# A two-layer attention and MLP kernel: second layer's key sums in one PSUM bank, held exponentials, last rows in the first pair, queries ahead of the last group, later first norm

## The chip, the cores and the metric

The kernel runs on one core of a Trainium2 chip. The metric is the device time of one execution in microseconds (us); the median of three runs stands for a version.

## The reference

Two layers, each of attention and MLP, on one sequence of S = 2048 rows and D = 576 columns, in float32. The attention is linear: queries and keys of H = 32 heads (18 columns each) go through a per-head matrix and two softmaxes, one of the products and one of their negatives.

```
q, k, v = layernorm(x) @ wqkv                     # per head, 18 columns
pq, pk  = q @ w_phi[h], k @ w_phi[h]
phi_q   = concat(softmax(pq), softmax(-pq))       # the same for phi_k
kv, z   = sum_s phi_k^T v, sum_s phi_k            # per head, over all rows
o       = (phi_q kv) / (phi_q z + 1e-6)
x       = x + concat_heads(o) @ wo
x       = x + relu(layernorm(x) @ w1 + b1)^2 @ w2 + b2     # F = 4608
```

This is done twice with the same weights. `kv` and `z` need the keys of all 2048 rows before any query can use them.

## The kernel before

The rows are four blocks of TB = 512, each of NT = 4 tiles of 128. The 576 columns are KC = 4 chunks of 128 and a rest of 64, the 4608 hidden columns NF = 36 groups of 128. Each float32 product is three matmuls on a high and a low part of both operands: ACT makes the high part by a rounding copy, DVE or POOL the low part by a subtraction. So most matmuls wait for a split, a `..h` tile of ACT and a `..l` tile of DVE or POOL.

The stages are these. `g_fold` multiplies wqkv's query and key columns by `w_phi` (tiles `fr`, `fp`, `ft`, `fo`), and the norm of block 0 is woven into it. `g_keys` makes values and keys of each block; `soft_parts`, `soft_exp`, `soft_sums` and `soft_scale` turn a tile of keys into two softmaxes (tile `k_..e`: maxima and minima and half of the differences on DVE, exponential on ACT, sums on DVE, the scaling by POOL, L495); `kv_tile` adds `phi_k^T v` of a tile in 32 small matmuls (L527). At the `barrier`, once all keys are in, `sums_operands` builds from `kv` the matrices with which queries are multiplied: `z`, then `kt` by groups of heads; the last group goes over `kq` (DVE, L580) and two matmuls (L585). Then come the other block's query projections (`g_q`), `g_phi` (sums and scaling of `phi_q`, L643 to L670) and `g_out` (its transposes `t0opt`, L716).

The MLP runs twice on one block (`g_mlp`) and once on a pair of blocks (`g_pair`). In `g_pair`, `products` makes the hidden columns of two blocks with fewer products (PSUM tiles `m_ppx`, `m_ppy`, `m_ppz`) and multiplies the first block's by `w2`; `seconds` does that for the second block in 36 sections of 15 matmuls (numbers 36 to 71: `m_pach`, `m_pacacc`, operands `m_ps` and `m_phc`). In layer 0 the second layer's norm, values and keys of three blocks are woven into `seconds` (`back_keys`; tiles `n_3`, `v_3`, `k_3`, then `_2`, then `_0`).

Eight PSUM banks: two of `ps_w`, and `acc0` to `acc4` and `h`. `wtile` hands out the two, and in turn with them those that `spare["tags"]` lists. For the first eight tiles of layer 1, `kv_tile` uses a `wtile` bank each and ACT or DVE adds it to `kv` (L533, L535); from then on it accumulates in `acc0`.

The code gives engines their work in one order, but a scheduling layer decides how each engine's queue is filled. `weave` runs two generators at a set rate, `held` and `tc.issue_after` keep instructions behind another one. A wait in an engine's queue holds all that stands behind it.

Of the kernel before, what the change touches and what calls it, by code (L numbers as in the profile page):

```python
# [7 lines left out]
F32 = mybir.dt.float32  # L8
# [5 lines left out]
P = 128  # L14
# [7 lines left out]
def layers_kernel(  # L22
# [96 lines left out]
    def paced(gen, cost):  # L119
        for own in gen:  # L120
            yield own if cost is None else cost

# [88 lines left out]
    def g_fold(kpair, vpair):  # L211
# [22 lines left out]
        def turn(k):  # L234
# [15 lines left out]
            nc.vector.tensor_copy(wt[:w, : n * P], pt[:w, : n * P])  # L250
# [84 lines left out]
    def g_norm(x_of, dst, name, then=None, fine=False):  # L335
# [4 lines left out]
        def scale(t):  # L340
            x = x_of(t)
            mv, rstd = moments(x, t, name)
            xn = sb.tile([P, KC * P], F32, tag="xn", name=f"{name}n{t}")
# [29 lines left out]
        def split_rest(h, pt):  # L373
# [3 lines left out]
            nc.vector.tensor_sub(xh[DT:, KC, rows], pt[DT:, : TB // 2], xh[DT:, KC, rows].bitcast(F32))  # L377
# [32 lines left out]
        for half in range(2):  # L410
            for t in range(2):
                apart(half * 2 + t)
                yield 2.2
            yield from pipeline(3, (lambda i: cross(half * 3 + i), lambda i: split(half * 3 + i)), (0.3, 0.6))
# [12 lines left out]
    def project(x, t, w, name):  # L427
# [6 lines left out]
        for k, (a, m) in enumerate(ops):  # L434
            nc.tensor.matmul(pt[:, :HP], a, m, start=(k == 0), stop=(k == len(ops) - 1))
# [73 lines left out]
    def kv_tile(layer, vt, e, name):  # L509
# [7 lines left out]
        first = 0 if layer == 0 else (NB - 2) * NT  # L517
        if n == first:
            st["ps"] = ps_a.tile([P, TB], F32, tag="acc0", name=f"kvp{layer}")
            nc.tensor.matmul(st["ps"][:, : 2 * NS * DH], zero, zeros, start=True, stop=True)  # L520
        stay, last = n >= first, n == NB * NT - 1
        pt = st["ps"] if stay else wtile(f"{name}k")
        po = pt[:, : 2 * NS * DH].rearrange("p (s j f) -> p s j f", s=2, f=DH)
        for j in range(NS):
            for q in range(NQ):
                h = head(q, j)
                nc.tensor.matmul(po[32 * q : 32 * q + 32, :, j], vt[:, h * VW : h * VW + 32],  # L527
                                 e[:, :, h * DH : (h + 1) * DH], start=not stay, stop=True,
                                 tile_position=(0, 32 * q), skip_group_check=True)
        if stay and not last:  # L530
            return
        if (last and first == 0) or n == 0:
            dense["evicted"] = nc.scalar.activation(kv, po, AF.Copy)  # L533
        else:
            nc.vector.tensor_add(kv, po, kv)  # L535

    def sums_operands(layer):
# [28 lines left out]
        for s in range(2):  # L566
# [10 lines left out]
        w = gw[last]  # L577
        own = sb.tile([P, TB], F32, tag="hr", name=f"kq{layer}", bufs=2)
        own = own[:, : 2 * w].rearrange("p (s q f) -> p s q f", s=2, q=NQ)
        nc.vector.tensor_mul(own, kv[:, :, HG].unsqueeze(2).to_broadcast([P, 2, NQ, DH]),  # L580
                             quarter.unsqueeze(1).unsqueeze(3).to_broadcast([P, 2, NQ, DH]))
        pt = wtile(f"kt{layer}2")
# [895 lines left out]
```

## Time and profile before

| | |
|---|---|
| runs | 2551.11, 2557.3, 2559.26 us; median 2557.3 |
| profiled execution | 2557.62 us, its span 2555.9 us |
| PE (TensorE matmul) busy | 2489.1 us, 97% |
| DVE, ACT, POOL busy | 64%, 51%, 38% |
| mean granted TensorE clock | 0.991 |

In the rows of a profile `kv_3k L527 <- POOL k_3K3e L495` means that the instruction of line 527 that writes `kv_3k` stood until POOL's instruction of line 495 that writes `k_3K3e` was done. A row of the timeline has start, duration, engine, line, operation, output <- inputs, shape and count, and in brackets the idle time before it with what ended it. Matmuls of one shape in sequence are merged.

### The profile page before, as it was taken

To read this page: it belongs to the slowest core of one execution; us is meant where nothing else is said; L and a number is where in the kernel's file an instruction comes from. 1 tells how busy PE (TensorE), PEld (TensorE's weight loads), DVE (VectorE), ACT (ScalarE), POOL (GpSimd) and SP (SyncE) were. 2 spreads that over 40 slices of the span, in tenths; PEclk is the share of its full clock that TensorE was granted. 3 is DMA by queue.
4 is the path that set the end of the run, shared out by engine and by line. 5 is a ranking of instruction groups with operands and counts; after the bars stand their busy time and mean duration, and the time that the engine had idled before them with its cause. 6 is when DMAs were issued, how large, how long until landed. Compare 5 with 4: busy or idle time off the path is not lost. (4 is left out here: it accounts for less than half of the span.)

```text
span 2555.9 us, 41504 instructions
## 1 busy us (share of the span) xinstructions
PE 2489.1 (97%) x15108; PEld 2182.6 (85%) x15108; DVE 1634.6 (64%) x2570; ACT 1304.2 (51%) x2293; POOL 971.8 (38%) x1101
## 2 busy tenths in 40 slices
PE   8998999999999999999999989999999999999999
PEld 7998888889888888888889988888888888888888
DVE  7777857555866655555777769484658665555444
ACT  4333555354546666664443435553545466666643
POOL 3544313212335555551434533032123445555322
PEclk9999999999999999999999999999999999999999
DMA  8102432344334433338543133333453344333363
GB/s 252 57 23 72 153 111 83 107 141 165 112 117 126 136 118 98 112 102 265 180 128 115 46 111 110 101 89 107 139 183 90 124 130 144 109 101 104 110 201 128
DMA packets 257224, 312.99 MB, mean 122 GB/s; under 512 B 29818, under 2 KB 175482, under 8 KB 254458
## 3 DMA queue, kind: packets, MB, share of 16 engines
q1 hardware_dynamic: 255760, 307.64, 38.7%
q8 instruction: 118, 1.93, 0.3%
q10 hardware_dynamic: 1258, 2.70, 0.3%
q14 instruction: 88, 0.72, 0.1%
HBM read 255.42 MB, written 54.82 MB: 121 GB/s over the span
## 5 line engine op out<-in xcount | busy, mean ns | idle before, releaser
L1118 POOL TENSOR_TENSOR m_ps<-m_pr,m_ps 128x128 fp32r<-128x128 f32 x144 | 121.9, 847 | 319.2 <-ACT m_ps L1116 264.8
L1117 DVE TENSOR_TENSOR m_ps<-m_pr,m_ps 128x448 fp32r<-128x448 f32 x144 | 93.9, 652 | 153.5 <-ACT m_ps L1116 151.2
L1157 PE MATMUL m_pacc<-m_ps,m_phb 128*128 128x448 f32 x864 | 188.5, 366 | 0.0
L1157 PEld LDWEIGHTS m_pacc<-m_ps,m_phb 128*128 128x128 f32 x864 | 162.2, 188 | 18.0
L1116 ACT ACTIVATE m_ps<-m_pr 128x576 fp32r<-128x576 f32 x144 | 97.9, 680 | 132.3 <-issue 88.5
L1157 PE MATMUL m_pacacc<-m_ps,m_phc 128*128 128x448 f32 x648 | 146.0, 369 | 0.0
L1157 PEld LDWEIGHTS m_pacacc<-m_ps,m_phc 128*128 128x128 f32 x648 | 123.3, 191 | 10.1
L1138 DVE TENSOR_TENSOR m_phb<-m_pz,m_phb 128x512 fp32r<-128x512 f32 x72 | 56.5, 784 | 115.9 <-ACT m_pz L1137 114.4
L820 PE MATMUL m_1ph<-t1onh,m_1h 128*128 128x512 f32 (+1 forms) x380 | 100.7, 390 | 4.5 <-ACT m_1hr L827 2.4
L820 PE MATMUL m_3ph<-t0onh,m_3h 128*128 128x512 f32 (+1 forms) x380 | 98.8, 386 | 2.8 <-ACT m_3hr L827 2.4
L847 PE MATMUL m_2acc<-m_2s,m_2hb 128*128 128x448 f32 x432 | 100.1, 365 | 0.0
L847 PE MATMUL m_0acc<-m_0s,m_0hb 128*128 128x448 f32 x432 | 100.1, 365 | 0.0
L847 PE MATMUL m_3acc<-m_3s,m_3hb 128*128 128x448 f32 x432 | 99.7, 366 | 0.0
L847 PE MATMUL m_1acc<-m_1s,m_1hb 128*128 128x448 f32 x432 | 99.7, 366 | 0.0
L820 PE MATMUL m_0ph<-a_0nh,m_0h 128*128 128x512 f32 (+1 forms) x380 | 97.7, 384 | 0.0
L820 PE MATMUL m_2ph<-a_2nh,m_2h 128*128 128x512 f32 (+1 forms) x380 | 97.7, 384 | 0.0
L847 PEld LDWEIGHTS m_2acc<-m_2s,m_2hb 128*128 128x128 f32 x432 | 81.0, 188 | 10.6 <-ACT m_2hb L828 0.2
L847 PEld LDWEIGHTS m_0acc<-m_0s,m_0hb 128*128 128x128 f32 x432 | 81.0, 188 | 10.7 <-ACT m_0hb L828 0.2
L847 PEld LDWEIGHTS m_3acc<-m_3s,m_3hb 128*128 128x128 f32 x432 | 81.0, 188 | 10.6 <-ACT m_3hb L828 0.2
L847 PEld LDWEIGHTS m_1acc<-m_1s,m_1hb 128*128 128x128 f32 x432 | 81.0, 188 | 10.5
L820 PEld LDWEIGHTS m_1ph<-t1onh,m_1h 128*128 128x128 f32 x380 | 70.2, 193 | 19.2 <-ACT m_1hr L827 3.2
L810 POOL TENSOR_TENSOR m_1s<-m_1r,m_1s 128x128 fp32r<-128x128 f32 x36 | 27.0, 749 | 151.7 <-ACT m_1s L806 134.8
(2504 smaller groups left out, 7464.3 us busy)
## 6 DMA issues: line engine op xcount, KB each, us to landing
m_pr<-in_B_w SPq DMA_DIRECT2D x144, 288.0 KB
m_pr<-in_B_w SPq DMA_DIRECT2D x72, 256.0 KB
hd<-m_pu SPq DMA_DIRECT2D x72, 256.0 KB
m_pg<-hd SPq DMA_DIRECT2D x72, 256.0 KB
m_3r<-in_B_w SPq DMA_DIRECT2D x36, 288.0 KB
m_2r<-in_B_w SPq DMA_DIRECT2D x36, 288.0 KB
m_1r<-in_B_w SPq DMA_DIRECT2D x36, 288.0 KB
m_0r<-in_B_w SPq DMA_DIRECT2D x36, 288.0 KB
```

The lines of the kernel that those rows point to most:

```text
L810: nc.gpsimd.tensor_sub(s2[:, D + R : 2 * D], r2[:, R:], s2[:, R:D].bitcast(F32))
L820: nc.tensor.matmul(ph[:, cols], a, m, start=(k == 0), stop=(k == len(ops) - 1))
L847: nc.tensor.matmul(acc[t][:, :R], a[:, rows], m, start=(f == 0 and k == 0), stop=(f == NF - 1 and k == 2))
L1116: nc.scalar.activation(s2[:, :D], r2, AF.Copy)
L1117: nc.vector.tensor_sub(s2[:, D : D + R], r2[:, :R], s2[:, :R].bitcast(F32))
L1118: nc.gpsimd.tensor_sub(s2[:, D + R : 2 * D], r2[:, R:], s2[:, R:D].bitcast(F32))
L1138: nc.vector.tensor_sub(hl, r, hh.bitcast(F32))
L1157: nc.tensor.matmul(accs[b][t][:, :R], a[:, rows], m, start=(g == 0 and k == 0), stop=(g == NF - 1 and k == 2))
```

## The change

It has seven parts. (1) In layer 1 all key sums accumulate in bank `acc4` from the first tile on, and ACT copies them out once; `acc4` is no longer handed out during `seconds` (behind it, `acc0` is handed out in its place). (2) In `back_keys` the sums of a tile come one tile later (`late`), and a block's last tile after the next block's norm; the norm makes all four tiles' scales first, in buffers of the tag `qk`; `g_features` keeps its exponentials behind the squares. (3) The first two steps of `back_keys`, two tiles of the first norm, are taken before the last rows of `products`. (4) The last group of `sums_operands` comes after all query projections. (5) In the first of the MLP's groups the low part of `m_1s` waits for the norm. (6) At the end of `g_mlp` the next stage's first products come ahead of the last rows. (7) The first norm starts three steps later in the weave, and behind the latest `ft` copy.

```diff
@@ -122,2 +122,6 @@
 
+    def idle(n, gen):
+        yield from (1.0 for _ in range(n))
+        yield from gen
+
     def lagged(n, produce, consume, by=1):
@@ -249,3 +253,3 @@
             wt = sb.tile([GW, TB], F32R, tag="ft", name=f"ft{c}_{i}", bufs=4).bitcast(F32)
-            nc.vector.tensor_copy(wt[:w, : n * P], pt[:w, : n * P])
+            dense["folded"] = nc.vector.tensor_copy(wt[:w, : n * P], pt[:w, : n * P])
             return wt
@@ -342,3 +346,6 @@
             mv, rstd = moments(x, t, name)
-            xn = sb.tile([P, KC * P], F32, tag="xn", name=f"{name}n{t}")
+            if fine:
+                xn = sb.tile([P, D], F32, tag="qk", name=f"{name}n{t}", bufs=5)[:, : KC * P]
+            else:
+                xn = sb.tile([P, KC * P], F32, tag="xn", name=f"{name}n{t}")
             nc.vector.tensor_scalar(xn, x[:, : KC * P], mv[:, 0:1], rstd, op0=ALU.subtract, op1=ALU.mult)
@@ -376,3 +383,4 @@
             nc.scalar.activation(xh[:, KC, rows], pt[:, : TB // 2], AF.Copy)
-            nc.vector.tensor_sub(xh[DT:, KC, rows], pt[DT:, : TB // 2], xh[DT:, KC, rows].bitcast(F32))
+            dense["normed"] = nc.vector.tensor_sub(xh[DT:, KC, rows], pt[DT:, : TB // 2],
+                                                   xh[DT:, KC, rows].bitcast(F32))
 
@@ -409,7 +417,6 @@
 
-        for half in range(2):
-            for t in range(2):
-                apart(half * 2 + t)
-                yield 2.2
-            yield from pipeline(3, (lambda i: cross(half * 3 + i), lambda i: split(half * 3 + i)), (0.3, 0.6))
+        for t in range(NT):
+            apart(t)
+            yield 2.2
+        yield from pipeline(3 * NT // 2, (cross, split), (0.3, 0.6))
 
@@ -434,3 +441,3 @@
         for k, (a, m) in enumerate(ops):
-            nc.tensor.matmul(pt[:, :HP], a, m, start=(k == 0), stop=(k == len(ops) - 1))
+            dense["projected"] = nc.tensor.matmul(pt[:, :HP], a, m, start=(k == 0), stop=(k == len(ops) - 1))
         return pt
@@ -516,9 +523,6 @@
         st["n"] += 1
-        first = 0 if layer == 0 else (NB - 2) * NT
-        if n == first:
-            st["ps"] = ps_a.tile([P, TB], F32, tag="acc0", name=f"kvp{layer}")
+        if n == 0:
+            st["ps"] = ps_a.tile([P, TB], F32, tag=f"acc{KC * layer}", name=f"kvp{layer}")
             nc.tensor.matmul(st["ps"][:, : 2 * NS * DH], zero, zeros, start=True, stop=True)
-        stay, last = n >= first, n == NB * NT - 1
-        pt = st["ps"] if stay else wtile(f"{name}k")
-        po = pt[:, : 2 * NS * DH].rearrange("p (s j f) -> p s j f", s=2, f=DH)
+        po = st["ps"][:, : 2 * NS * DH].rearrange("p (s j f) -> p s j f", s=2, f=DH)
         for j in range(NS):
@@ -527,10 +531,6 @@
                 nc.tensor.matmul(po[32 * q : 32 * q + 32, :, j], vt[:, h * VW : h * VW + 32],
-                                 e[:, :, h * DH : (h + 1) * DH], start=not stay, stop=True,
+                                 e[:, :, h * DH : (h + 1) * DH], start=False, stop=True,
                                  tile_position=(0, 32 * q), skip_group_check=True)
-        if stay and not last:
-            return
-        if (last and first == 0) or n == 0:
+        if n == NB * NT - 1:
             dense["evicted"] = nc.scalar.activation(kv, po, AF.Copy)
-        else:
-            nc.vector.tensor_add(kv, po, kv)
 
@@ -576,15 +576,20 @@
 
-        w = gw[last]
-        own = sb.tile([P, TB], F32, tag="hr", name=f"kq{layer}", bufs=2)
-        own = own[:, : 2 * w].rearrange("p (s q f) -> p s q f", s=2, q=NQ)
-        nc.vector.tensor_mul(own, kv[:, :, HG].unsqueeze(2).to_broadcast([P, 2, NQ, DH]),
-                             quarter.unsqueeze(1).unsqueeze(3).to_broadcast([P, 2, NQ, DH]))
-        pt = wtile(f"kt{layer}2")
-        p3 = pt[:w, : 2 * w].rearrange("p (s n) -> p s n", s=2)
-        for s in range(2):
-            nc.tensor.matmul(p3[:, s], own[:, s].rearrange("p q f -> p (q f)"),
-                             place.rearrange("p q d -> p (q d)"), start=True, stop=True)
-        keep(p3, [k[:w, :, last, :w] for k in (kbh, kbl)])
         sums[layer].update(zb=zb, kb=(kbh, kbl))
 
+        def last_group():
+            w = gw[last]
+            own = sb.tile([P, TB], F32, tag="hr", name=f"kq{layer}", bufs=2)
+            own = own[:, : 2 * w].rearrange("p (s q f) -> p s q f", s=2, q=NQ)
+            nc.vector.tensor_mul(own, kv[:, :, HG].unsqueeze(2).to_broadcast([P, 2, NQ, DH]),
+                                 quarter.unsqueeze(1).unsqueeze(3).to_broadcast([P, 2, NQ, DH]))
+            pt = wtile(f"kt{layer}2")
+            p3 = pt[:w, : 2 * w].rearrange("p (s n) -> p s n", s=2)
+            with tc.issue_after(dense["projected"].ins):
+                for s in range(2):
+                    nc.tensor.matmul(p3[:, s], own[:, s].rearrange("p q f -> p (q f)"),
+                                     place.rearrange("p q d -> p (q d)"), start=True, stop=True)
+            keep(p3, [k[:w, :, last, :w] for k in (kbh, kbl)])
+
+        return last_group
+
 
@@ -688,3 +693,3 @@
         yield from held(pipeline(NT, (start, lambda t: soft_exp(ph[t]), add, factors, lambda t: phi_scale(ph[t], rs[t])),
-                                 (2.6, 0.4, 3.0, 2.8, 1.2)))
+                                 (2.6, 0.4, 3.0, 2.8, 1.2)), ("last", "squared"))
 
@@ -808,2 +813,3 @@
                 nc.vector.tensor_sub(l1, r1, h1.bitcast(F32))
+            with tc.issue_after(dense["normed"].ins) if behind else nullcontext():
                 nc.vector.tensor_sub(s2[:, D : D + R], r2[:, :R], s2[:, :R].bitcast(F32))
@@ -878,2 +884,8 @@
         nc.scalar.activation(yt, acc[KC], AF.Copy)
+        if then:
+            then()
+        for t in range(NT):
+            x = sb.tile([P, D], F32, tag="x", name=f"{name}x{t}", bufs=5)
+            nc.sync.dma_start(x, xm[b][t])
+            after.append(x)
         by_rows(NF - 1, range(2), range(3))
@@ -883,9 +895,2 @@
             nc.tensor.transpose(p3[:, t], yt[:, t * P : (t + 1) * P], ident)
-        for t in range(NT):
-            x = sb.tile([P, D], F32, tag="x", name=f"{name}x{t}", bufs=5)
-            nc.sync.dma_start(x, xm[b][t])
-            nc.vector.tensor_add(x[:, R:], p3[:, t], x[:, R:])
-            after.append(x)
-        if then:
-            then()
         by_rows(NF - 1, range(2, NT), range(3))
@@ -893,2 +898,4 @@
             nc.vector.tensor_add(x[:, :R], acc[t][:, :R], x[:, :R])
+        for t, x in enumerate(after):
+            nc.vector.tensor_add(x[:, R:], p3[:, t], x[:, R:])
             nc.sync.dma_start(out[b * TB + t * P : b * TB + (t + 1) * P] if layer else xs[b][t], x)
@@ -1335,3 +1342,3 @@
         drain(softs)
-        sums_operands(layer)
+        last_group = sums_operands(layer)
         spare["tags"] = [f"acc{i}" for i in range(NC)] + ["h"]
@@ -1344,2 +1351,3 @@
         drain(queries)
+        last_group()
         dst = {}
@@ -1353,3 +1361,3 @@
     vpair = [piece_tiles(f"w0v{h}", TAGS_A) for h in range(2)]
-    weave(g_fold(kpair, vpair), g_norm(load_x(0), xT[0], "n0_0"), 0.5)
+    weave(g_fold(kpair, vpair), idle(3, held(g_norm(load_x(0), xT[0], "n0_0"), ("folded",))), 0.5)
     pending = []
@@ -1405,2 +1413,3 @@
             new_slots("vs")
+            late = []
             for b in order[:3]:
@@ -1410,2 +1419,5 @@
                 yield from g_norm(rows_of(b), xk, f"n{m}", fine=True)
+                while late:
+                    kv_tile(1, *late.pop(0))
+                    yield 0.8
                 if not last:
@@ -1425,6 +1437,10 @@
 
-                stages = (raw, start, lambda t: soft_exp(es[t]), end, lambda t: None)
-                if not last:
-                    stages += (lambda t: kv_tile(1, vts[t], es[t], f"kv{m}_{t}"),)
-                yield from pipeline(NT, stages, (1.0, 2.6, 0.4, 1.8, 0.1, 0.8))
+                def keep_sums(t):
+                    if not last:
+                        late.append((vts[t], es[t], f"kv{m}_{t}"))
+                        if len(late) > 1:
+                            kv_tile(1, *late.pop(0))
+
+                yield from pipeline(NT, (raw, start, lambda t: soft_exp(es[t]), end, keep_sums),
+                                    (1.0, 2.6, 0.4, 1.8, 0.8))
                 if last:
@@ -1440,5 +1456,8 @@
         weave(g_mlp(layer, order[1], nxt, [], f"m{layer}_{order[1]}", None, then), back, 5.0)
-        drain(products)
-        spare["tags"] = ["acc4"]
-        weave(seconds, iter(()) if layer else back_keys(), 4.0)
+        back = iter(()) if layer else back_keys()
+        for k, _ in enumerate(products):
+            if k == NP - 1:
+                next(back, None)
+                next(back, None)
+        weave(seconds, back, 4.0)
         if layer == 0:
@@ -1446,3 +1465,3 @@
             prev, b = order[-2], order[-1]
-            spare["tags"] = ["acc1", "acc2", "acc3", "acc4", "h"]
+            spare["tags"] = ["acc0", "acc1", "acc2", "acc3", "h"]
             x, xprev, vpair = {}, keep["x"], keep["v"]
```

The order that the scheduler makes differs at many places. Three of them follow. Line numbers are those of each kernel (the changed one's are 4 to 7 higher around here).

PE, barrier of layer 0. `t0q2qp` are query projections, `t0opt` the first transposes of `g_out`. Before:

```order
L435 MATMUL t0q2qp_2895<-t0q0h,n_2h 128x288
L435 MATMUL t0q2qp_2895<-t0q0h,n_2l 128x288 x4
L435 MATMUL t0q2qp_2895<-t0q0l,n_2h 128x288 x2
L585 MATMUL kt_2797<-place,kq_2795 72x72 x2
L435 MATMUL t0q2qp_2832<-t0q1h,n_2h 128x288 x5
L435 MATMUL t0q2qp_2832<-t0q1h,n_2l 128x288 x4
```

Now:

```order
L442 MATMUL t0q2qp_2937<-t0q1h,n_2h 128x288 x5
L442 MATMUL t0q2qp_2937<-t0q1h,n_2l 128x288 x4
L442 MATMUL t0q2qp_2937<-t0q1l,n_2h 128x288 x5
L589 MATMUL kt_2955<-place,kq_2953 72x72 x2
L721 MATMUL t0opt_2982<-ident,t0fQ0e 126x128
L721 MATMUL t0opt_2982<-ident,t0fQ1e 126x128
```

The two `kt` matmuls went from the middle of the projections to their end.

PE and DVE in `seconds`, at the end of the second layer's first block of keys. `k_3K3e` is that block's last tile of exponentials, `n_2` the next block's norm, `w_2v` its value weights; numbers 48 and 49 are sections. PE before:

```order
L527 MATMUL kv_3_2k<-k_3K2e,vs_12028 32x2x18 x32
L527 MATMUL kv_3_3k<-k_3K3e,vs_12029 32x2x18 x32
L1157 MATMUL m_pach<-m_ps_48_12670,m_phc_12676 128x448 x3
L1157 MATMUL m_pacacc_11963<-m_ps_48_12670,m_phc_12676 128x448 x3
L1157 MATMUL m_pacacc_11964<-m_ps_48_12670,m_phc_12676 128x448 x3
```

PE now:

```order
L376 MATMUL n_2p_12949<-ident,n_2e 128x128 x2
L1164 MATMUL m_pacacc_12003<-m_ps_49_12772,m_phc_12778 128x448 x3
L1164 MATMUL m_pacacc_12004<-m_ps_49_12772,m_phc_12778 128x448 x3
L1154 MATMUL m_pacacc_12005<-m_phc_12778,m_ps_49_12772 128x512 x3
L362 MATMUL n_2p_12980<-ident,n_2n_12891 128x128 x4
L362 MATMUL n_2p_12987<-ident,n_2n_12904 128x128 x4
L531 MATMUL kvp_12669<-k_3K3e,vs_11923 32x2x18 x32
L1164 MATMUL m_pach<-m_ps_50_12857,m_phc_12863 128x448
```

DVE before:

```order
L1117 TENSOR_TENSOR m_ps_48_12670<-m_pr_48_12668,m_ps_48_12670 128x448
L1202 TENSOR_TENSOR m_phc_12676<-m_pg_12674,m_phc_12676 128x512
L309 TENSOR_TENSOR w_2v0l<-w_2v0r,w_2v0h 128x1440
L309 TENSOR_TENSOR w_2v1l<-w_2v1r,w_2v1h 128x1440
L470 TENSOR_REDUCE k_3K3m<-k_3ks_12624 128x32
L471 TENSOR_REDUCE k_3K3m<-k_3ks_12624 128x32
L474 TENSOR_TENSOR k_3K3e<-k_3ks_12624,k_3K3m 128x576
L1117 TENSOR_TENSOR m_ps_49_12735<-m_pr_49_12733,m_ps_49_12735 128x448
```

DVE now:

```order
L478 TENSOR_REDUCE k_3K3m<-k_3ks_12598 128x32
L481 TENSOR_TENSOR k_3K3e<-k_3ks_12598,k_3K3m 128x576
L351 TENSOR_SCALAR n_2n_12891<-x_2_2_12881,n_2m_12884,n_2d_12885 128x512
L1124 TENSOR_TENSOR m_ps_48_12709<-m_pr_48_12707,m_ps_48_12709 128x448
L1209 TENSOR_TENSOR m_phc_12715<-m_pg_12713,m_phc_12715 128x512
L352 TENSOR_SCALAR n_2e<-x_2_2_12881,n_2m_12884,n_2d_12885 128x128
L334 BN_AGGR n_2m_12897<-n_2s_12896 128x2
L313 TENSOR_TENSOR w_2v1l<-w_2v1r,w_2v1h 128x1440
L490 TENSOR_REDUCE k_3K3r<-k_3K3e 128x64
L1124 TENSOR_TENSOR m_ps_49_12772<-m_pr_49_12770,m_ps_49_12772 128x448
L491 RECIPROCAL k_3K3r<-k_3K3r 128x64
L1209 TENSOR_TENSOR m_phc_12778<-m_pg_12776,m_phc_12778 128x512
```

On PE the sums of the last tile moved from ahead of section 48 to ahead of section 50, behind the next norm's transposes. On DVE the splits of sections 48 and 49 now stand behind three scales `n_2n` (two more come just before the rows shown), and one of the two weight splits, and the key steps.

DVE, start of the kernel. `ft` are copies that the fold's matmuls read, `n_0s` the statistics of the first norm on the loaded `x`. Before:

```order
L250 COPY ft_0_221<-fp_0_216 126x512
L329 BN_STATS n_0s_226<-x_0_0_224 128x6 x2
L250 COPY ft_1_242<-fp_1_237 126x512
L330 BN_AGGR n_0m_227<-n_0s_226 128x2
L250 COPY ft_2_247<-fp_2_244 72x256
```

Now:

```order
L254 COPY ft_0_221<-fp_0_216 126x512
L254 COPY ft_1_228<-fp_1_223 126x512
L254 COPY ft_2_233<-fp_2_230 72x256
L254 COPY ft_0_251<-fp_0_246 126x512
L254 COPY ft_1_268<-fp_1_263 126x512
L277 TENSOR_TENSOR w0k0l<-fo_1_253,w0k0h 128x288
L277 TENSOR_TENSOR w0k1l<-fo_2_270,w0k1h 128x72
L254 COPY ft_2_284<-fp_2_281 72x256
L254 COPY ft_0_303<-fp_0_298 126x512
L333 BN_STATS n_0s_318<-x_0_0_316 128x6
```

The first statistics moved behind six more copies and two splits.

## The prediction

> **What bounds the kernel now.** The page comes first: which engine fills the span.
>
> ```profile
> PE 2489.1 (97%) x15108; PEld 2182.6 (85%) x15108; DVE 1634.6 (64%) x2570; ACT 1304.2 (51%) x2293; POOL 971.8 (38%) x1101
> ```
>
> PE (TensorE) works 2489.1 of 2555.9 us, so at most 66.8 us can be won without taking away a matmul. The change takes away hardly any: only PE's pauses can pay. The table of waits names them (total us, times, longest).
>
> ```profile
> PE kt L585 <- DVE kq L580: 7.4, 2, 4.4
> PE kv_3k L527 <- POOL k_3K3e L495: 6.1, 1, 6.1
> PE kv_3k L527 <- POOL k_2K3e L495: 5.0, 1, 5.0
> PE fo L259 <- DVE ft L250: 3.8, 3, 3.1
> PE m_ppx L1128 <- DVE m_pu L1241: 2.8, 2, 1.4
> PE n_3p L355 <- DVE n_3n L344: 2.3, 1, 2.3
> PE n_0p L355 <- DVE n_0n L344: 2.0, 3, 1.5
> PE a_1qp L435 <- ACT a_1qs L453: 1.5, 1, 1.5
> PE m_1ph L820 <- DVE m_1h L808: 1.4, 1, 1.4
> PE z L547 <- DVE kv L535: 0.8, 1, 0.8
> ```
>
> All but the `a_1qp` row lie where the change moves something; those nine rows sum to 31.6 us. A pause costs more than its length: the table of busy time by stretch (PE, PEld, DVE, ACT, POOL, then the granted clock) shows PE at half clock right after the long ones.
>
> ```profile
> 206.21:209.62 3.41, 3.02 (x14) 3.02 (x15) 3.41 (x9) 0.29 (x1) 0.17 (x1) 0.50 0.75 212
> 1469.14:1472.55 3.41, 3.25 (x15) 3.25 (x16) 3.41 (x10) 0.70 (x2) 0.00 (x0) 0.50 0.00 0
> 1250.68:1254.10 3.42, 3.34 (x70) 3.05 (x71) 2.71 (x5) 0.00 (x0) 1.69 (x3) 0.50 0.44 126
> 1326.79:1332.60 5.81, 5.81 (x77) 5.26 (x78) 2.62 (x5) 0.00 (x0) 1.61 (x2) 0.50 0.61 172
> ```
>
> Work at half clock loses about half its busy time: 1.5, 1.6, 1.7 and 2.9 us, together 7.7.
>
> **The change part by part.**
>
> *Queries ahead of the last group.* In both barriers PE stood before the two `kt` products.
>
> ```profile
> 204.30 2.25 DVE L580 TENSOR_TENSOR kq<-kv,quarter 128x144 f32<-128x144 f32 x1
> 206.60 0.75 PE L585 MATMUL kt<-place,kq 128*72 128x72 f32 x4 [4.38 <-DVE kq L580]
> 213.32 1.68 POOL L662 TENSOR_TENSOR t0fQ1e<-t0fQ1e,t0fQ1r 128x576 f32<-128x576 f32 x1 [0.84 <-DVE t0fQ1r L657]
> 217.95 0.27 PE L716 MATMUL t0opt<-ident,t0fQ0e 128*126 128x128 f32 x1
> 1469.30 0.76 PE L585 MATMUL kt<-place,kq 128*72 128x72 f32 x4 [3.06 <-DVE kq L580]
> 1476.02 1.68 POOL L662 TENSOR_TENSOR t1fQ1e<-t1fQ1e,t1fQ1r 128x576 f32<-128x576 f32 x1 [0.84 <-DVE t1fQ1r L657]
> 1481.16 0.27 PE L716 MATMUL t1opt<-ident,t1fQ0e 128*126 128x128 f32 x1
> ```
>
> The query projections no longer queue behind `kt`, so PE reaches `t0opt` earlier by wait and slow clock, 4.38 + 1.5 = 5.9, at 212.05. What ends last there next is POOL's scaling of `t0fQ1e`, done at 215.00. The 2.25 us `kq` leaves the DVE chain ahead of it, so I put it at 212.75: gain 5.2. In layer 1 `kq` was short, the scaling (1477.70) moves only some 0.3 to 1477.4, and the gain is 1481.16 - 1477.4 = 3.75. Sum **9.0**; if POOL's scaling did not move at all, 2.95 + 3.46 = 6.4; gross, 10.6.
>
> *Held exponentials and the key sums in one bank.* At two block ends PE waited for the last tile's scaled exponentials and got 6.06 + 1.7 and 5.03 + 2.9 us late: 15.7. Now that tile's sums come after the next block's norm, so nothing of it is on PE's way. But DVE was full there too (12.07 of 12.70 us), and it splits the operands of PE's next sections (15 matmuls each, `m_pach` first).
>
> ```profile
> 1232.00:1244.70 12.70, 12.70 (x244) 10.74 (x242) 12.07 (x12) 7.36 (x12) 4.89 (x4) 1.00 0.49 142
> 1235.98 2.64 DVE L1202 TENSOR_TENSOR m_phc<-m_pg,m_phc 128x512 fp32r<-128x512 f32 x1
> 1238.54 1.91 DVE L309 TENSOR_TENSOR w_2v0l<-w_2v0r,w_2v0h 128x1440 fp32r<-128x1440 f32 x1
> 1241.95 0.74 DVE L470 TENSOR_REDUCE k_3K3m<-k_3ks 128x32 f32<-128x576 f32 x1
> 1243.93 1.58 DVE L1117 TENSOR_TENSOR m_ps<-m_pr,m_ps 128x448 fp32r<-128x448 f32 x1
> 1245.44 0.94 DVE L1202 TENSOR_TENSOR m_phc<-m_pg,m_phc 128x512 fp32r<-128x512 f32 x1
> 1246.30 1.34 DVE L483 TENSOR_REDUCE k_3K3r<-k_3K3e 128x64 f32<-128x1152 f32 x1
> 1248.38 2.33 POOL L495 TENSOR_TENSOR k_3K3e<-k_3K3e,k_3K3r 128x1152 f32<-128x1152 f32 x1 [2.54 <-DVE k_3K3r L484]
> 1249.11 2.14 DVE L1202 TENSOR_TENSOR m_phc<-m_pg,m_phc 128x512 fp32r<-128x512 f32 x1
> 1250.76 1.19 PE L527 MATMUL kv_3k<-k_3K3e,vs 128*32 128x36 f32 x64 [6.06 <-POOL k_3K3e L495]
> 1252.34 0.68 DVE L1202 TENSOR_TENSOR m_phc<-m_pg,m_phc 128x512 fp32r<-128x512 f32 x1
> 1256.76 0.55 DVE L344 TENSOR_SCALAR n_2n<-x,n_2m,n_2d 128x512 f32<-128x512 f32 x1 [3.38 <-PE n_2p L355]
> ```
>
> By the new order the split at 1235.98 serves section 47, not 48, and three `n_2n` of 0.55 us stand ahead of section 48's. From 1238.54 on: two `n_2n`, one `w_2v0l` (some 1.9), three key steps of 0.74, a third `n_2n`: 5.8, so `m_ps_48` starts near 1244.3 and `m_phc_48` ends near 1246.2. PE, busy up to 1244.70, wants both there: the sums of tiles 0 to 2 only change places with sections 45 to 47. That returns 1.5. Section 49 hangs on a `w_2v1l`, the 1.34 reduction, two short steps and an `m_phc` that falls on POOL's 2.33 us scaling: 0.68 alone, 2.14 beside POOL, so 0.9 to 2.4 is returned. Midway, about 3.2 of 7.8 comes back; the second block end has the same pieces, and with a little for what a late DVE pushes on I take 7 of 15.7 back and keep **8.7**. Bounds: nothing returned, 15.7; 6.3 returned at each end, 3. The eight DVE additions `kv` (L535) go free. The last one, `z`'s 0.85, becomes an ACT copy behind four matmuls: **0.4** (0 to 0.85).
>
> *Last rows in the first pair.* `n_3n` of two tiles is now made before `last_rows`, so the 2.31 us at `n_3p` go. Its other two tiles now stand ahead of the `m_px` additions, which free the banks for section 36.
>
> ```profile
> 1169.81 1.67 DVE L1183 TENSOR_TENSOR m_px<-m_pacc,m_px 128x448 f32<-128x448 f32 x3
> ```
>
> `x_3_3` is loaded only when `x_3_2`'s buffer is free, and DVE stands before its statistics. I reckon these additions start some 0.6 us later than now and PE waits that long: **1.7** kept (0 to 2.3). Behind that load SP's queue holds the weights of section 38 and `w_3v0r`, wanted two sections and more later; I cost this at nothing, and at the same 0.6 again if that cover is gone.
>
> *MLP parts.* The `m_1h` split moves ahead of `m_1s`: **1.4** (0 to 2.9, if the slow clock behind it goes as well). At the end of `g_mlp` all four tiles' products stand between two `m_ppx` groups, 12 matmuls (the row below has six) and four transposes, where 1.40 + 1.41 us were needed: **2.8** for the two layers (1.4 to 2.8). The exponentials that `g_features` now holds behind the squares cost nothing on an ACT that is 51% busy; if a query tile's sums come late by it, the weave has other matmuls there, and I see no wait on them in the table above.
>
> ```profile
> 855.44 1.40 PE L847 MATMUL m_2acc<-m_2s,m_2hb 128*128 128x448 f32 x6
> 9.80 0.82 DVE L329 BATCH_NORM_STATS2 n_0s<-x 128x6 f32<-128x288 f32 x2 [3.82 <-DMA x<-in_A_x]
> ```
>
> *Later first norm.* DVE stood 3.82 us before the statistics of `x` while the `ft` copies that PE wanted were queued behind them. Six more copies now come first. The waits in this stage beyond kernel start are about 3.8 + 2.0 plus small ones; the norm ends later and may hold the first projections, so I take **4.0** of some 6.6 (-2 to 6.6).
>
> Sum: 9.0 + 8.7 + 0.4 + 1.7 + 1.4 + 2.8 + 4.0 = 28.0. The profiled execution took 2557.62 (span 2555.9 and 1.7 around it), 0.3 above the median; 2557.3 - 28.0 = **2529.3**.
>
> **A rule against a row.** The Trainium skill, page "TensorE: Matmul & The Clock Gate", section "What's actually happening", says the clock halves after at least one idle window of about 3.4 us. The trace is stricter: after the 3.06 us wait at 1469.30, shorter than that, the clock was 0.50. By the rule that place would lose no 1.6 us and layer 1's `kt` would gross 3.06; that is below the 3.75 I take, so the sum would be 27.3 and the time 2530.0.
>
> **The rivals.** *Half of it: DVE and POOL set the pace* (0.20). For it: DVE was 12.07 of 12.70 busy, and its `m_phc` took 2.64 and 2.14 beside POOL's scaling against 0.68 alone. Against it: DVE idled 3.38 us soon after (row at 1256.76). Then `kt` gives 6.4, the block ends 3, `m_ppx` 2.8, the rest nothing: 12.2, or 2545. The Trainium skill, page "SBUF — State Buffer", section "SBUF: two separate sides", has DVE operations with two SBUF inputs and GpSimd ones hold a shared port for a whole instruction, the later one fully blocked. The 2.14 beside a 2.33 agrees; by that rule the larger return (2.4, not 0.9) holds at section 49.
>
> *Slower: two banks instead of three.* `acc4` leaves the rotation in layer 0's second products, so each of the 40 projections (16 values, 24 keys) takes the bank that the last but one left, and needs ACT's eviction. The `a_1qp` row shows one such wait, 1.5 us, though just one in the kernel. Projections in this stage never waited with three banks. At 1.5 each it is 60 us and the time 2557.3 - 28 + 60 = 2589. It decides from 28/40 = 0.7 a projection: 0.08. At 0.5 to 0.9 each (20 to 36) the result is within 0.3% of before: 0.10.
>
> **How the numbers follow.** A measurement of this kernel can tell 0.3%, 7.7 us. Forecast 0.62, half 0.20 (also faster), no change 0.10, slower 0.08: faster 0.82, same 0.10, slower 0.08. My own case runs from the upper bounds (10.6 + 15.7 + 0.85 + 2.3 + 2.9 + 2.8 + 6.6 = 41.8: 2516) to 2543, where half of the sum is left and the half rival starts; that rival's spread reaches 2549. Range 2517 to 2549.
>
> **What would show it.** Right: `kt` gone from the waits, and what is left at `t0opt` under 1 us with POOL as releaser; no `kv_3k` wait; new waits of `m_pach` on DVE `m_phc` or `m_ps` of 2 to 4 us at each block end; clock 1.00 there; `n_3p` under 1 us; no `m_ppx` wait on L1248; `fo` under 1 us. Wrong: `v_2pv` or `k_2kp` waiting for ACT's evictions again and again (two banks), `m_pach` waiting over 5 us at a block end, or the first `v_0pv` waiting for `n_0h`.

## The result

The changed kernel took 2539.8 us (median of five runs, 2535.8 to 2546.4) against 2557.3 for the kernel before: a ratio of 0.9937, 95% interval 0.9917 to 0.9958. The interval excludes 1, so it is faster, as forecast, and it is inside the range; but the gain is 17.5 us and not 28.0. The profiled execution took 2540.98, its span 2539.3.

The first page row and, of the waits of PE in the changed kernel, those that bear on the argument (total us, times, longest):

```profile
PE 2486.9 (98%) x15108; PEld 2183.0 (86%) x15108; DVE 1641.5 (65%) x2562; ACT 1307.5 (51%) x2293; POOL 968.9 (38%) x1101
PE n_2p L376 <- DVE n_2l L371: 5.8, 1, 5.8
PE t1onp L362 <- DVE t1onn L351: 4.4, 4, 2.0
PE m_ppx L1135 <- DVE m_pu L1244: 3.4, 4, 1.4
PE n_0p L362 <- DVE n_0n L351: 2.6, 1, 2.6
PE n_0p L376 <- DVE n_0l L371: 2.1, 1, 2.1
PE t0opt L721 <- DVE t0fQ0e L667: 1.2, 1, 1.2
PE t1opt L721 <- DVE t1fQ0e L667: 1.2, 1, 1.2
PE kt L589 <- DVE kq L583: 1.2, 2, 0.7
```

PE's idle time went from 66.8 to 52.4 us. Gone are both long `kt` waits, the two `kv_3k` waits and `m_1h`. But the longest wait, 5.8 us, is new, and none of the predicted `m_pach` waits is there.

Where the time went is read from when named matmuls start. The table takes the start of one matmul after another in each trace; a negative number is time won in that stretch. The second profile is one of the same kernel, taken later (`x8_after_again`).

| stretch, from the start of one matmul to that of the next | forecast | first profile | second |
|---|---|---|---|
| start to the first `z` of layer 0 (fold, first norm, keys) | -4.0 | +0.3 | +1.8 |
| to the first `m_3acc` (barrier, `kt`, `t0opt`) | -5.2 | -0.7 | -3.6 |
| to the first `m_2acc` (MLP with `g_features` beside it) | 0 | -4.6 | -4.6 |
| to the first `m_pacc` (end of `g_mlp`, `products`) | -1.4 | -1.9 | -1.7 |
| to section 36 | 0 | -0.2 | -0.2 |
| to the first `k_3kp` (last rows, first norm of stage) | -1.7 | -3.2 | -3.0 |
| to the first `n_lastp` (both block ends) | -8.7 | -0.5 | -2.1 |
| to layer 1's last `z` row | -0.4 | -1.6 | -1.6 |
| to the first `m_1acc` (barrier, `kt`, `t1opt`, `m_1h`) | -5.2 | +0.8 | +2.7 |
| to the last `m_1acc` (MLP with `g_features`) | 0 | -4.6 | -4.6 |
| to the end | -1.4 | -0.3 | -0.9 |

So the largest gain, 9.2 us, is one costed at nothing, and the two largest terms, 9.0 and 8.7, brought about 0 to 2 each.

### The profile page after: what moved, and what is told of

Same layout as the page of the kernel before. It is cut to its first block, busy times and chain, and to the rows that moved or that the text cites. A ratio compares the mean times of both kernels' runs of the same rounds, so it can differ in the third digit from the quotient of the medians.

```text
span 2539.3 us, 41497 instructions
## 1 busy us (share of the span) xinstructions
PE 2486.9 (98%) x15108; PEld 2183.0 (86%) x15108; DVE 1641.5 (65%) x2562; ACT 1307.5 (51%) x2293; POOL 968.9 (38%) x1101
## 5 line engine op out<-in xcount | busy, mean ns | idle before, releaser
L853 PEld LDWEIGHTS m_0acc<-m_0s,m_0hb 128*128 128x128 f32 x432 | 80.9, 188 | 10.6 <-ACT m_0hb L834 0.2
L853 PEld LDWEIGHTS m_2acc<-m_2s,m_2hb 128*128 128x128 f32 x432 | 80.9, 188 | 10.6 <-ACT m_2hb L834 0.2
L816 POOL TENSOR_TENSOR m_0s<-m_0r,m_0s 128x128 fp32r<-128x128 f32 x36 | 29.6, 824 | 143.5 <-ACT m_0s L811 127.4
L816 POOL TENSOR_TENSOR m_2s<-m_2r,m_2s 128x128 fp32r<-128x128 f32 x36 | 29.2, 810 | 143.5 <-ACT m_2s L811 136.7
```

The lines of the kernel that those rows point to most:

```text
L816: nc.gpsimd.tensor_sub(s2[:, D + R : 2 * D], r2[:, R:], s2[:, R:D].bitcast(F32))
L853: nc.tensor.matmul(acc[t][:, :R], a[:, rows], m, start=(f == 0 and k == 0), stop=(f == NF - 1 and k == 2))
```

## The experiments

**The gain that was costed at nothing.** In the kernel before, ACT's queue (start, duration; in brackets the idle time before) stood at the exponential of a query tile until POOL had made its input. Behind it stood the squares' first step `m_3hr`, for which PE waited:

```profile
429.67 1.16 ACT L479 ACTIVATE a_0Q3e<-a_0Q3e 128x1152 f32<-128x1152 f32 x1 [6.15 <-POOL a_0Q3e L475]
430.74 0.67 ACT L827 ACTIVATE m_3hr<-m_3ph,b1t 128x512 f32<-128x512 f32 x1
431.46 2.50 PE L820 MATMUL m_3ph<-t0onh,m_3h 128*128 128x512 f32 x5 [2.36 <-ACT m_3hr L827]
431.60:435.00 3.40, 3.40 (x9) 2.68 (x10) 2.58 (x4) 2.16 (x4) 0.90 (x1) 0.51 0.22 64
```

The last row is the table by stretch: 3.4 us at clock 0.51 behind the wait, which costs 1.7 more. Layer 1 has the same at 1697.75. In PE's list of waits before, the two are these rows, which the prediction's table leaves out although it shows shorter ones:

```profile
PE m_1ph L820 <- ACT m_1hr L827: 2.4, 1, 2.4
PE m_3ph L820 <- ACT m_3hr L827: 2.4, 1, 2.4
```

With `("last", "squared")` ACT does the squares first, and in the profile of the changed kernel neither wait nor slow stretch is left. Two runs test this, one without that edit and one with it alone.

`x1_no_exps`: the change without

```diff
-                                 (2.6, 0.4, 3.0, 2.8, 1.2)), ("last", "squared"))
+                                 (2.6, 0.4, 3.0, 2.8, 1.2)))
```

> The changed kernel with one thing undone: g_features no longer keeps its exponentials behind the squares (all else as changed). Theory (ACT's queue): before, the exponential a_0Q3e stood 6.15 us in ACT's queue waiting for POOL, and m_3hr behind it made PE wait 2.36 us in each layer, with a half-clock stretch after it; the changed kernel gained 4.6 us between the 180th and the 300th m_3acc matmul and again 4.6 us at m_1acc in layer 1. So both waits on ACT L833 of about 2.4 us come back, both gains of 4.6 go, and the time is 9 us above the changed kernel's 2540: about 2549. Rival (the pause went because the low split of m_3s was put behind the norm): no wait comes back and the time stays within 2 us of 2540.

2547.1 us, ratio to before 0.9957 (0.9941 to 0.9974), 7.3 above the change. Both waits are back, 2.4 us each, and the two MLP stretches win less than 0.1 us each instead of 4.6:

```profile
PE m_3ph L826 <- ACT m_3hr L833: 2.4, 1, 2.4
PE m_1ph L826 <- ACT m_1hr L833: 2.4, 1, 2.4
```

`x2_exps_alone`: the kernel before with that line alone.

> The kernel before with one edit of the change: g_features holds its exponentials behind the squares. Theory (the exponential of a query tile stood in ACT's queue waiting 6.15 us for POOL, with the squares of the MLP features behind it): both waits of PE on m_3hr and m_1hr, 2.36 us each, go and the 3.4 us of half clock behind each; 4.5 us in each layer, about 9 in all, 2548. Rival, as the prediction had it (these exponentials are worth nothing): 2556 to 2557, and the gain of 5 us between m_3acc's 180th and 300th matmul in the profile of after came from another edit.

2548.5 us, ratio 0.9967 (0.9954 to 0.998): 7.4 us. In its trace the two stretches win 4.6 and 4.7 us. The edit is worth 9.2 in its own stretches and 7 to 7.5 in the medians; that is about 40% of what the whole change brought.

**The new wait at the block end.** The third norm's transposes stood 5.82 us. They need one of the two banks in the rotation, and DVE's split `n_2l` frees it. DVE's queue in the changed kernel, with one row of POOL and PE's row:

```profile
1238.54 2.47 POOL L502 TENSOR_TENSOR k_3K3e<-k_3K3e,k_3K3r 128x1152 f32<-128x1152 f32 x1 [1.18 <-DVE k_3K3r L491]
1238.92 2.37 DVE L351 TENSOR_SCALAR n_2n<-x,n_2m,n_2d 128x512 f32<-128x512 f32 x1
1241.47 1.17 DVE L333 BATCH_NORM_STATS2 n_0s<-x 128x6 f32<-128x288 f32 x3
1242.67 0.76 DVE L333 BATCH_NORM_STATS2 n_0s<-x 128x6 f32<-128x288 f32 x2
1244.86 1.12 DVE L333 BATCH_NORM_STATS2 n_0s<-x 128x6 f32<-128x288 f32 x3
1248.18 1.29 DVE L371 TENSOR_TENSOR n_2l<-n_2p,n_2h 128x512 fp32r<-128x512 f32 x2
1248.93 0.69 PE L376 MATMUL n_2p<-ident,n_2e 128*128 128x128 f32 x2 [5.82 <-DVE n_2l L371]
```

Statistics of the next block (`n_0s`, 3.05 us of eight) and the splits of later sections came before `n_2l`. Ahead of them `n_2n` took 2.37 us beside POOL's scaling of 2.47, where it took 0.55 in the kernel before. Two remedies: give the third bank back, or hold the statistics back.

`x4_three_banks`: the key sums and `spare["tags"]` as in the kernel before.

```diff
+        first = 0 if layer == 0 else (NB - 2) * NT
...
+        spare["tags"] = ["acc4"]
         weave(seconds, back, 4.0)
```

> The changed kernel with the key sums of the second layer's first two blocks made as before, each in a bank of the rotation and added to kv by DVE, so that the rotation has three banks (acc4 back); the held last tile and the late sums stay. Theory (bank): the waits of n_2p and n_0p tail transposes on DVE's n_2l and n_0l (5.82 and 2.12 us in the changed kernel, with half clock after them) go, below 1 us each; the first value projection v_2pv comes 6 us earlier relative to k_3 than in the changed kernel, and 8 to 11 us are won in all: 2529 to 2532. Rival (DVE sets the pace): a wait of 3 us or more at each block end stays, now of m_pach on m_ps or m_phc; the time is 2535 to 2540.

2528.5 us in one run. The 5.8 us became 2.8 and, at the next transposes, 1.2; DVE's addition into `kv` now ends the longer one. The block ends' stretch won 4.5 us.

```profile
PE n_2p L376 <- DVE kv L542: 2.8, 1, 2.8
```

But 4.8 us of its gain lies elsewhere, at layer 1's barrier, which the bank theory doesn't explain; it is taken up below.

`x5_stats_held`: two banks, but

```diff
+            with tc.issue_after(dense["normed"].ins) if fine else nullcontext():
                 mv, rstd = moments(x, t, name)
```

> The changed kernel, still with two banks in the rotation, with the statistics of a block's rows kept behind the last split of the block ahead (in the changed kernel 3.4 us of n_0s statistics stand in DVE's queue ahead of the n_2l that frees the bank). Theory (the bank wait is as long as what DVE does ahead of n_2l): the 5.82 us wait falls by about 3.4 to some 2.4, one half-clock stretch less; 3.5 to 5 us are won at the first block end, less at the second. Rival (the wait hangs on something else, the exponentials' scaling or the splits): it stays above 5 us.

2531.5 us in one run; the block ends win 5.9, and the wait is 2.9 us:

```profile
PE n_2p L377 <- DVE n_2l L372: 2.9, 2, 2.7
```

So the statistics ahead of `n_2l` are at least as good a cause as the bank: without them half of the wait goes, with the bank back about a third. The totals of these two runs hold more than that: at layer 0's barrier, which neither edit touches, they win 5.7 and 5.8 us, against 0.7 and 3.6 in the two profiles of the change.

`x9_banks_and_stats`: both.

> The change with both remedies for the wait of the third norm's transposes: three banks in the rotation, with the key sums kept as before, and the norm's statistics held behind the split that frees a bank. Theory (both take away the same wait, that of n_2p and n_0p on n_2l and n_0l): their gains of about 11 and 8 us do not add, 2525 to 2530. Rival (they are separate gains): 2520 or less.

2526.7 us, ratio 0.9882 (0.9866 to 0.9898): the gains don't add, as expected. The block ends win 6.0 us. At the second one `n_0p` still waits 2.6 us for `n_0l`; what is left of the wait at the first is released by DVE's addition into `kv`:

```profile
PE n_2p L377 <- DVE kv L543: 1.7, 1, 1.7
```

**The barrier.** `x3_kt_early` puts the last group back ahead of the queries:

```diff
-        last_group = sums_operands(layer)
+        sums_operands(layer)()
```

Its two `kt` matmuls also lose the `tc.issue_after` that keeps them behind the projections.

> The changed kernel with the last group of kt put back ahead of the query projections in both barriers. Theory (the gain is given back inside the barrier): PE waits 3 to 4.4 us at kt again, but the second half of g_out (tiles Q2, Q3) hangs on DVE and POOL, which do not start earlier for it; by the first m_3acc matmul of layer 0 the kernel stands within 1 us of the changed one, in layer 1 within 2 us. Rival, the prediction's term: the move is worth 9 us, so 5 us are lost in layer 0 by the first m_3acc and 4 us more in layer 1, time about 2549.

2544.8 us in one run, between the two. In layer 0 this kernel wins 0.9 us in the stretch and in layer 1 it loses 3.0; over both that is 2 to 3 us worse than the two profiles of the change. So inside the change the move is worth 2 to 3 us by the stretches and 5 by the whole time, not 9; 2.0 us of the loss against the first profile lie ahead of layer 0's first `z`, where the edit changes nothing. The `kt` waits grew to 5.7 and 5.8 us, against 4.38 and 3.06 in the kernel before:

```profile
PE kt L588 <- DVE kq L583: 11.4, 2, 5.8
```

So something else in the change had made DVE late here. Layer 1 in the change, POOL, DVE, ACT and PE:

```profile
1446.52 0.41 ACT L535 ACTIVATE kv<-kvp 128x288 f32<-128x288 f32 x1 [0.45 <-PE kvp L531]
1448.20 1.15 ACT L312 ACTIVATE t1oo0h<-t1oo0r 126x1152 fp32r<-126x1152 f32 x1
1449.42 3.95 POOL L313 TENSOR_TENSOR t1oo0l<-t1oo0r,t1oo0h 126x1152 fp32r<-126x1152 f32 x2 [2.33 <-ACT t1oo0h L312]
1451.89 0.82 DVE L652 TENSOR_TENSOR t1fm<-t1fQ0e,zb 128x576 f32<-128x576 f32 x1
1452.63 7.91 DVE L563 TENSOR_TENSOR kbl<-ko,kbh 126x504 fp32r<-126x504 f32 x2
1453.33 2.68 POOL L313 TENSOR_TENSOR t1oo1l<-t1oo1r,t1oo1h 126x1152 fp32r<-126x1152 f32 x1
1466.71 0.30 PE L721 MATMUL t1opt<-ident,t1fQ0e 128*126 128x128 f32 x1 [1.19 <-DVE t1fQ0e L667]
```

and before:

```profile
1456.80 1.16 ACT L308 ACTIVATE t1oo0h<-t1oo0r 126x1152 fp32r<-126x1152 f32 x1
1458.03 3.39 POOL L309 TENSOR_TENSOR t1oo0l<-t1oo0r,t1oo0h 126x1152 fp32r<-126x1152 f32 x2
1465.34 3.69 DVE L563 TENSOR_TENSOR kbl<-ko,kbh 126x504 fp32r<-126x504 f32 x2
```

`g_out` issues its weights' conversions behind `dense["evicted"]`. In the kernel before, the last writer of that key in layer 1 was the eviction of a value tile; now it is the ACT copy of the finished key sums, so the conversion stands after the copy instead of before. POOL's four splits slid with it: with two multiplications `t1fm` between them, POOL was busy without a pause beside DVE's two `kbl` subtractions, which took 7.91 instead of 3.69 us, and `t1opt` stands behind those. In layer 0 the copy had been on ACT in the kernel before too. `x4_three_banks` undid this in layer 1 without meaning to, which is its 4.8 us there. The test is one line:

`x10_pieces_early`

```diff
-            dense["evicted"] = nc.scalar.activation(kv, po, AF.Copy)
+            nc.scalar.activation(kv, po, AF.Copy)
```

> The change with one edit: the ACT copy of the finished key sums no longer stands as the instruction behind which g_out issues the conversions of its weights (L312), so that they stand behind the last eviction of a value tile, as in layer 1 of the kernel before. Theory (in the change ACT's t1oo0h and POOL's t1oo splits moved behind the copy, and POOL's 7.4 us of them now fall on the two kbl subtractions of DVE, 7.91 us instead of 3.69; t1opt stands behind these): the two kbl take about 3.7 to 4.5 us in both layers, the waits of t0opt and t1opt on Q0e (1.19 us each) go, and the kt sites are 4 to 6 us earlier in layer 1 and 2 to 5 in layer 0; 2531 to 2535. Rival, as the prediction had it (POOL's scaling of Q1e sets t0opt and t1opt): nothing moves by more than 1 us, 2538 to 2541.

2531.1 us, ratio 0.9898 (0.988 to 0.9916): 8.7 us less than the change. Layer 1 again:

```profile
1440.90 3.39 POOL L313 TENSOR_TENSOR t1oo0l<-t1oo0r,t1oo0h 126x1152 fp32r<-126x1152 f32 x2
1442.35 2.05 PE L547 MATMUL z<-kv,top 128*128 128x126 f32 x16 [1.08 <-ACT kv L535]
1446.58 4.50 DVE L652 TENSOR_TENSOR t1fm<-t1fQ0e,zb 128x576 f32<-128x576 f32 x1
1451.00 1.27 DVE L563 TENSOR_TENSOR kbl<-ko,kbh 126x504 fp32r<-126x504 f32 x2
1460.68 0.33 PE L721 MATMUL t1opt<-ident,t1fQ1e 128*126 128x128 f32 x1 [0.58 <-POOL t1fQ1e L667]
```

The two `kbl` are down to 1.27 us, though the multiplication ahead of them now meets POOL (4.50): together 5.77 us instead of 8.73. The waits on `t0fQ0e` and `t1fQ0e` are gone, and the barriers win 6.6 and 4.5 us. The price is at layer 1's first `z`, which waits 1.08 us because ACT's copy of the sums now stands behind the conversion. The other profiles bear this out. In layer 1 the five with early pieces (`x4`, `x9` to `x12`) win 3.4 to 4.8 us at the barrier, while the seven of changed kernels with late ones lose 0.2 to 3.1. In layer 0 `x10` to `x12` win 6.6 to 7.3, the other changed kernels 0.7 to 5.8. What ends last at `t1opt` is now POOL's scaling, as the prediction had said.

**The smaller terms.** `x6_norm0_old` takes the first norm's delay back:

```diff
-    weave(g_fold(kpair, vpair), idle(3, held(g_norm(load_x(0), xT[0], "n0_0"), ("folded",))), 0.5)
+    weave(g_fold(kpair, vpair), g_norm(load_x(0), xT[0], "n0_0"), 0.5)
```

> The change with the first norm as before, neither held behind the folded copies nor delayed. Theory (the later first norm brings nothing: the waits of fo on ft move to waits of n_0p on n_0n, and the clock is halved for longer): the fold ends as early as with it or up to 1 us earlier, less slow clock around 29 to 36 us, total the same to 3 us less than after (2537 to 2540). Rival, as the prediction had it (the later first norm is worth 4.0 us): 2544.

2536.7 us, ratio 0.9919 (0.9903 to 0.9935): no slower than the change. The wait of `fo` is back at 3.9 us, but in the change its place had been taken, one step on, by `n_0p`, behind POOL's splits:

```profile
26.90 0.79 POOL L285 TENSOR_TENSOR w0v0l<-fv,w0v0h 128x288 fp32r<-128x288 f32 x1
27.66 0.22 POOL L335 TENSOR_SCALAR n_0d<-n_0m 128x1 f32<-128x1 f32 x1
28.57 1.00 DVE L351 TENSOR_SCALAR n_0n<-x,n_0m,n_0d 128x512 f32<-128x512 f32 x1 [1.53 <-POOL n_0d L336]
29.71 1.08 PE L362 MATMUL n_0p<-ident,n_0n 128*128 128x128 f32 x4 [2.55 <-DVE n_0n L351]
28.90:32.30 3.40, 2.58 (x13) 2.58 (x14) 3.37 (x8) 1.02 (x4) 0.39 (x1) 0.50 0.89 245
```

The first `v_0pv` started at 36.0 to 37.9 us in the nine profiles with the later norm and at 35.0 to 37.7 in the five with the old one; the first `k_0p`, behind the values of the first tile, at 40.3 to 42.2 against 38.7 to 41.5. The delay brings nothing and may cost 1 us.

`x7_no_lastrows` drains the last rows first, as before:

```diff
+        drain(products)
-        for k, _ in enumerate(products):
-            if k == NP - 1:
-                next(back, None)
-                next(back, None)
```

> The change without the early start of the third stage's norm: the last rows are drained first and the norm of section 36's block is not begun ahead of them. Theory, as the prediction had it in sign: the 2.3 us wait of n_3p comes back and the stretch from section 36 to k_3 is 2 to 3.3 us longer (2542 to 2543). Rival (that gain came from the held key sums of the same stretch): the stretch keeps its length to 0.5 us.

2538.9 us in one run, no slower than the change. The stretch to `k_3kp` wins 0.5 instead of 3.0 to 3.2 us, with `n_3p` waiting 1.9 in all, so the edit does bring 2.6 us there. But the block ends then win 2.6 instead of 0.5 to 2.1: part of it is lost again at waits that come later anyway. One run can't say how much is left.

**The same kernel again.** `x8_after_again` is the changed kernel, unaltered.

> The changed kernel unaltered, profiled a second time. Theory (where PE pauses for about the same time, whether its clock is then halved for 3.4 or 6.8 us, or not at all, differs from one execution to the next): the list of waits is the same to 0.3 us a row, but the stretch from the end of layer 0's keys to the first product of m_3 differs from the first profile's by 2 us or more, and the stretch before the last layer's m_1 likewise. Rival (the clock follows from the waits alone): the two profiles agree to 0.5 us at each of these places.

2539.6 us. The two barriers differ from the first profile by 2.9 and 1.9 us (the latter just short of the 2 expected), but not by the clock alone: in layer 0 the list of waits differs too. Half clock from 195.2 to 198.6 made the `z` products 3.62 us instead of 1.99, all that follows came later, POOL's splits had moved on, and the `kbl` pair took 4.48 instead of 7.77:

```profile
195.15 3.62 PE L547 MATMUL z<-kv,top 128*128 128x126 f32 x16
202.18 4.48 DVE L563 TENSOR_TENSOR kbl<-ko,kbh 126x504 fp32r<-126x504 f32 x2 [0.43 <-ACT kbh L562]
215.78 0.33 PE L721 MATMUL t0opt<-ident,t0fQ1e 128*126 128x128 f32 x1 [0.58 <-POOL t0fQ1e L667]
```

The waits of 1.19 and 0.92 us that the first profile has there are gone. Losing 1.6 us early won more than that later.

**All remedies.** `x11_one_bank_best` is the change with the edits of `x5`, `x6` and `x10`; `x12_three_banks_best` has the old key sums and three banks besides.

> The change with three remedies at once: the pieces of g_out behind the last value eviction, the statistics of the third stage's norm behind the split that frees a bank, and the first norm as before. Key sums in one bank, two banks in the rotation, as in the change. Theory (three separate places: about 8.6, 5 at the norm without what the pieces bring, and 0 to 3): 2522 to 2527. Rival (they share their gain): 2528 to 2531.

> The same three remedies, and besides the key sums and the banks as in the kernel before: three banks in the rotation, DVE's additions into kv. Theory (the held exponentials and their late sums are what counts at the block ends, the one bank saves only the 0.85 us before z and costs a bank that the norm's transposes want): 2 to 5 us less than with one bank, 2518 to 2523. Rival (with the statistics held back, two banks are enough): within 2 us of it, or slower by the additions on DVE.

2526.9 us, ratio 0.9877 (0.9863 to 0.9892), and 2524.7 us, ratio 0.9869 (0.9852 to 0.9885). The first is within what was expected of three separate places, but at its upper end and 1.1 us short of the rival's; the second is 1.7 above what was expected, and its lead of 2.2 us lies in the overlap of the two intervals. Whether the one bank costs anything once statistics and pieces are in place is left open. Both beat the change; the best is 32.5 us under the kernel before. PE's busy time fell by 11.7 us for the same 15108 matmuls, slow clock that is no longer there:

```profile
PE 2477.4 (98%) x15108; PEld 2172.8 (86%) x15108; DVE 1638.0 (65%) x2570; ACT 1305.4 (52%) x2293; POOL 968.7 (38%) x1101
```

## Why the prediction was right, and where it was not

The direction and the range were right, the sum was not: errors of opposite sign partly cancelled. Without the gain that was costed at nothing the time is 2547.1 (`x1_no_exps`), near the slow end of the range, so that the forecast came as near as it did is in part luck. By its own steps:

- *`kt` and the queries, 9.0.* The mechanism was right: `kt` left the path, and without the collision POOL's scaling of `Q1e` ends last. With the pieces early the barriers win 6.6 + 4.5 = 11.1 (`x10_pieces_early`; bounds 6.4 to 10.6, but the 4.5 holds the part of `m_1h`, and layer 0 gains beyond the kernel before, where the pieces were late too). In the change they win 0.7 to 3.6 in layer 0 and nothing in layer 1. The step that failed is the one on the "ACT copy behind four matmuls: 0.4": it priced the copy by its own length and didn't ask what stood behind `dense["evicted"]`. The order of the instructions would have shown L312 moving behind the copy.
- *The copy before `z`, 0.4.* The stretch to `z` won 1.6; with the pieces early nothing of it is left.
- *Block ends, 8.7 kept of 15.7.* The `kv_3k` waits went as said, and DVE did give it back, but more than the upper bound of 6.3 at each end: only 0.5 to 2.1 us was kept. The place was wrong too. The splits of sections 48 and 49 came in time; the norm's transposes `n_2p` and `n_0p` waited instead. The two-bank rival watched ACT's evictions of projections, 0.7 us each; no such wait is in the list. The bank mattered where DVE frees it.
- *Held exponentials of `g_features`, 0.* Measured 9.2 in its stretches. "I see no wait on them in the table above" asked the wrong question: the wait was on `m_3hr` and `m_1hr`, which stood behind them in ACT's queue, and the table above had left out just those two rows of 2.4 us. ACT at 51% had room; its order was the cost.
- *Last rows, 1.7.* 3.0 to 3.2 in the stretch, 2.6 of it by this edit; the predicted 0.6 at `m_px` is there (0.65 at 1164.92). Part is lost later.
- *`m_1h`, 1.4.* The wait went; `t1onp` waits now 4.4 us in all where it had 3.1. Not told apart from the barrier's loss.
- *`m_ppx`, 2.8.* Layer 0's stretch wins 1.7 to 1.9 (1.4 forecast). Layer 1's wins 0.3 to 0.9 up to the end. The two waits that it priced are gone; the four shorter ones behind another line of `m_pu` (L1237 before, L1244 now) are 2.2 us in all before and 3.4 and 2.1 in the two profiles.
- *First norm, 4.0.* Nothing, or a loss of up to 1: the wait moved to `n_0p`. Inside the bounds (-2 to 6.6), at the end that the text had named.
- *Half rival, 2545.* It had the right limit, DVE beside POOL, for the block ends and for the barrier, but not the gain that made up for it.

## What to carry to other kernels

An engine's queue is read in both directions: an instruction that waits costs whatever stands behind it, so a long idle stretch before an ACT or DVE row is followed to the next row of that queue and to who waits for that, however idle the engine is on average. When a change gives a name that others order themselves by (here `dense["evicted"]`) a new writer, every user of it moves too, and the order of the instructions shows this before any run. A PSUM bank taken from a rotation is paid for where the slowest reader frees it, which need not be the place where the rotation turns most often.

## What was not expected of the hardware

The clock does not follow from the waits alone. At layer 0's barrier `x1_no_exps` and the first profile of the change have nearly the same waits (0.44, 1.19, 0.92, 0.58 and 0.42, 1.19, 0.92, 0.33 us) before the same matmuls. Busy time by stretch (PE, PEld, DVE, ACT, POOL, clock), first the change, then `x1_no_exps`:

```profile
209.76:213.17 3.41, 1.80 (x14) 1.37 (x12) 3.38 (x9) 2.38 (x5) 1.20 (x1) 1.00 0.32 87
213.18:216.58 3.40, 2.15 (x10) 1.68 (x10) 1.99 (x6) 1.18 (x4) 3.12 (x4) 0.50 0.00 0
216.59:219.99 3.40, 3.40 (x18) 3.40 (x17) 1.90 (x5) 1.39 (x4) 2.12 (x2) 0.50 0.00 0
```

```profile
210.73:214.14 3.41, 1.78 (x15) 1.44 (x13) 3.38 (x8) 2.45 (x5) 1.20 (x1) 1.00 0.32 87
214.15:217.55 3.40, 1.89 (x15) 1.52 (x15) 2.14 (x6) 1.32 (x4) 3.03 (x4) 1.00 0.00 0
217.56:220.96 3.40, 3.40 (x32) 3.40 (x31) 3.17 (x10) 2.88 (x9) 2.23 (x2) 1.00 0.01 2
```

One ran 6.8 us at half clock, the other none. The rows are cut along a grid: in each of the fourteen profiles all changes of the clock lie whole multiples of 3.413 us apart, and this grid lies differently against the kernel in each. With every profile cut along its own grid, all 59 windows at full clock in which PE was busy for less than 43% were followed by half clock, none of the 9932 above 61%, and 34 of the 104 between. So what counted in these traces is how much of one such window PE stood idle, and where the windows begin decides how a wait is shared out between two of them. In the range between, where the first rows here lie (53% and 52%), the traces don't tell what decides.

Over eight profiles of kernels whose code between `z` and the first `m_3acc` is the same, that stretch won between 0.7 and 5.8 us, by the clock and by where POOL's splits met DVE: one profile is no measure of a barrier to better than some 5 us. The rule of the Trainium skill, page "TensorE: Matmul & The Clock Gate", section "What's actually happening", that at least one idle window of about 3.4 us precedes the half clock is not what these traces show, if idle means without any work: a wait of 2.36 us was followed by 0.51 at 431.6, and waits of 0.42 and 1.19 us, in a window with 1.80 us of work, by the 0.50 above.

The second surprise is how far a DVE operation on two SBUF operands is stretched beside POOL: a pair of `kbl` took 1.27 us with POOL idle and 7.91 beside POOL's full queue, with nothing in its row but its length to show for it, since a stretched instruction counts as busy and not as waiting.
